# Causal masks written into PSUM ahead of the scores, 256 or 512 columns at a time, in the opening of an attention and SwiGLU kernel

## Chip, cores, metric

One core of one Trainium2 chip. The metric is the device time of one execution in microseconds. The kernel before takes 338.25 us (median of three runs, 337.61 to 338.68). All runs used below are marked fast, with a mean granted TensorE clock of 0.993 to 1.000 in the records.

## The reference, cut to what matters

```python
B, H, S, D = 8, 8, 576, 64
scores = (1 / sqrt(D)) * q @ k.T          # per batch and head
rel = pos[:, None] - pos[None, :]
scores = where((rel >= 0) & (rel < 64), scores, -1e9)
attn = softmax(scores) @ v
x = attn as (B*S, H*D) = (4608, 512)
out = (silu(x @ w_gate) * (x @ w_val)) @ w_out      # 512 -> 1536 -> 512
```

A query sees itself and the 63 keys before it. The kernel works in 36 groups of 128 tokens. For each half of a group (64 queries) it multiplies against 128 keys, and a mask removes the keys outside the window.

## The kernel before: the parts that matter

The scores of a group lie in two PSUM banks, one for the even and one for the odd heads (`a`); the two use the upper and the lower 64 rows of the TensorE array. In seven groups of the opening (0, 2, 3, 5, 4, 7, 6, in this order) the mask is added by TensorE (`masked=True`): a matmul of a 64x128 table of 0 and -1e30 against an identity. In the other 29 groups VectorE multiplies the exponentials by 0 and 1 instead.

```python
def scores(g, masked=False):
    ps = [ps_a.tile([P, 4, 2, 64], FP32, name="s_ps", tag="a") for _ in range(2)]
    for b in range(2):
        o = P * (g % 2) + 64 * b
        for p in range(4):
            for a in range(2):
                ...                                     # keys, rows y of half a
                nc.tensor.matmul(
                    ps[a][:, p, b], keys, qT[g // 2 % QR][y, p, o:o + 64],
                    tile_position=(64 * a, 0), start=True, stop=not masked)
            if masked:
                for a in range(2):
                    y = slice(64 * a, 64 * a + 64)
                    m = minus[1 if ORDER[g][1] == 0 and b == 0 else 0]
                    nc.tensor.matmul(
                        ps[a][:, p, b], m[y], identb[y, y],
                        tile_position=(64 * a, 0), start=False, stop=True)
...
def keys_last(n):                # VectorE; waits for the transposed keys (a DMA)
    b, i = ORDER[2 * n]
    if i is None:
        dve.tensor_copy(kL[:, :, b:b + 4, 64:P], kT[n % KR]...)
...
scores(0, True); scores(1); load_vg(1); ...; load_vg(2); load_vg(3)
... warm(7) ...                  # filler matmuls
# main loop, second half of an iteration
turn1(n + 4, "k_f"); keys_before(n + 4); keys_last(n + 4)
project(t - 1, s) ... step(t, 3 * s + 2)
```

The softmax here doesn't subtract the row's maximum and nothing guards it: scores larger than these inputs give would overflow.

## Time and profile before

| | before |
|---|---|
| median of three runs | 338.25 us |
| span of the profiled run | 336.9 us |
| TensorE matmuls, weight loads | 2825, 2825 |
| mask matmuls of 64 columns | 112 |

### The profile page before, as it was taken

The page shows a single profiled execution, that of the slowest core. Times are in us where ns is not written, and L with a number is a line of the kernel's source. Part 1 is how long each engine was busy: PE and PEld are TensorE (multiplying, and loading weights), DVE is VectorE, ACT ScalarE, POOL GpSimd, SP SyncE. Part 2 cuts the span into 40 slices and gives each one's busy share as a digit, 9 for nine tenths or more (in the row PEclk, how much of TensorE's full clock was granted, in tenths as well). Part 3 has the DMA queues.
Part 4 walks back from the last instruction along what each step waited for, and adds up shares of the span by engine and source line. Part 5 has one row for each costly group of instructions (what it writes and reads, how often), then busy time and mean ns, then how long its engine had stood idle before and what let it go on. Part 6 is the DMA issues. An engine that isn't in the chain of part 4 may idle for free.

```text
span 336.9 us, 7388 instructions
## 1 busy us (share of the span) xinstructions
PE 327.6 (97%) x2825; PEld 164.1 (49%) x2825; DVE 226.3 (67%) x491; ACT 151.9 (45%) x268; POOL 100.5 (30%) x148
## 2 busy tenths in 40 slices
PE   7898999999999999999999999999999999999996
PEld 3555665555544444444444444444444444444444
DVE  4657889895676666666676767766667766655520
ACT  3766876664634343434343443434343434233222
POOL 4444356660053333333333333223333200000000
DMA  8999999998978999798879798999787720211013
GB/s 209 247 312 264 280 301 326 322 185 194 228 137 149 192 151 190 151 193 162 181 151 194 137 195 174 158 179 181 158 180 157 104 62 34 65 31 31 33 47 109
DMA packets 150612, 56.85 MB, mean 169 GB/s; under 512 B 124721, under 2 KB 144561, under 8 KB 150577
## 3 DMA queue, kind: packets, MB, share of 16 engines
q1 hardware_dynamic: 150576, 56.38, 77.5%
q8 instruction: 22, 0.36, 0.5%
q14 instruction: 14, 0.11, 0.2%
HBM read 37.75 MB, written 9.44 MB: 140 GB/s over the span
## 4 chain that ended last, share of the span: by engine, by line
PE 87%; DMA 8%; SPq 3%; ACT 1%; POOL 0%; issue 0%; ACTq 0%; POOLq 0%
PE g_ps L309 27%; PE o_ps L327 27%; PE v_ps L309 26%; DMA q_f<-in_q_dram 6%; PE ao_ps L245 3%; PE s_ps L207 3%; DMA v_f<-in_v_dram 2%; SPq L110 1%; SPq L89 1%; PE tp L170 1%; DMA out_dram<-os__4994 1%; PE xtp L269 0%; POOL q_fb L120 0%; ACT q_fb L118 0%; ACT os__4994 L332 0%
## 5 line engine op out<-in xcount | busy, mean ns | idle before, releaser
L309 PE MATMUL g_ps<-xT,wg 128*128 128x512 bf16 (+1 forms) x460 | 112.4, 367 | 0.2
L309 PE MATMUL v_ps<-xT,wv 128*128 128x512 bf16 (+1 forms) x460 | 112.1, 366 | 0.5 <-ACT wv L118 0.5
L320 DVE SCALAR_TENSOR_TENSOR sg<-th,g_ps 128x512 f32<-128x512 f32 (+1 forms) x115 | 75.0, 652 | 53.8 <-ACT th L314 53.5
L314 ACT ACTIVATE th<-g_ps 128x512 f32<-128x512 f32 (+1 forms) x115 | 65.9, 573 | 76.4 <-PE g_ps L309 73.6
L327 PE MATMUL o_ps<-wo,hT 128*128 128x512 bf16 (+2 forms) x456 | 98.5, 368 | 0.0
L321 DVE TENSOR_TENSOR hT<-sg,v_ps 128x512 bf16<-128x512 f32 (+1 forms) x115 | 75.4, 656 | 11.9 <-PE xtp L269 0.5
L309 PEld LDWEIGHTS <-wv 128*128 128x128 bf16 x460 | 44.7, 98 | 49.4 <-ACT wv L118 1.0
L327 PEld LDWEIGHTS <-hT 128*128 128x128 bf16 x456 | 43.6, 98 | 49.5
L309 PEld LDWEIGHTS <-wg 128*128 128x128 bf16 x460 | 41.8, 98 | 42.3 <-issue 0.6
L227 ACT ACTIVATE E<-s_ps 128x512 bf16<-128x512 f32 x72 | 38.5, 596 | 8.0 <-PE s_ps L207 8.0
L120 POOL CAST q_fb<-q_f 128x1024 bf16<-128x1024 f32 x13 | 13.6, 1044 | 64.9 <-DMA q_f<-in_q_dram 41.2
L120 POOL CAST k_fb<-k_f 128x1024 bf16<-128x1024 f32 (+1 forms) x16 | 16.0, 1003 | 56.1 <-DMA k_f<-in_k_dram 46.1
L256 DVE TENSOR_TENSOR x_b<-ao_ps,r 128x256 bf16<-128x256 f32 x72 | 30.6, 425 | 2.5
L120 POOL CAST ve<-v_f 64x512 bf16<-64x512 f32 x47 | 28.9, 615 | 2.9
L229 DVE TENSOR_TENSOR E<-E,mask 128x512 bf16<-128x512 bf16 x58 | 23.3, 427 | 9.1 <-ACT E L227 8.3
L120 POOL CAST vo<-v_f 128x512 bf16<-128x512 f32 x30 | 18.9, 630 | 30.3 <-DMA v_f<-in_v_dram 30.1
L255 DVE RECIPROCAL r<-ao_ps 128x4 f32<-128x4 f32 x72 | 12.6, 174 | 5.4 <-PE ao_ps L245 5.3
L245 PEld LDWEIGHTS <-E 128*64 128x64 bf16 x576 | 11.0, 110 | 7.8 <-issue 5.7
L207 PEld LDWEIGHTS <-kT 64*128 64x128 bf16 x512 | 10.1, 95 | 6.6 <-issue 4.0
L120 POOL CAST vL<-v_f 64x512 bf16<-64x512 f32 x15 | 9.6, 638 | 10.2 <-DMA v_f<-in_v_dram 9.5
L207 PE MATMUL s_ps<-qT,kT 64*128 64x64 bf16 x512 | 12.2, 191 | 0.4 <-DVE x_b L256 0.3
L245 PE MATMUL ao_ps<-ve,E 128*64 128x65 bf16 x256 | 11.9, 196 | 0.1
(100 smaller groups left out, 150.1 us busy)
## 6 DMA issues: line engine op xcount, KB each, us to landing
v_f<-in_v_dram SPq DMA_DIRECT2D x32, 256.0 KB, 4.6
k_f<-in_k_dram SPq DMA_DIRECT2D x20, 256.0 KB, 4.1
q_f<-in_q_dram SPq DMA_DIRECT2D x18, 256.0 KB, 4.7
q_f<-in_q_dram SPq DMA_DIRECT2D x7, 512.0 KB, 7.0
k_f<-in_k_dram SPq DMA_DIRECT2D x6, 512.0 KB, 7.6
w_f<-in_moe_w_gate_dram SPq DMA_DIRECT2D x6, 512.0 KB, 6.2
w_f<-in_moe_w_val_dram SPq DMA_DIRECT2D x6, 512.0 KB, 6.5
wo_f<-in_moe_w_out_dram SPq DMA_DIRECT2D x6, 512.0 KB, 7.3
```

The costliest lines, as they stand in the source:

```text
L120: eng.tensor_copy(y, x)
L207: nc.tensor.matmul(ps[a][:, p, b], keys, qT[g // 2 % QR][y, p, o:o + 64], tile_position=(64 * a, 0), start=True, stop=not masked,)
L227: act.activation(e, x[:], AF.Exp, scale=0.125)
L229: dve.tensor_mul(e, e, mk[:].unsqueeze(1).to_broadcast([P, 4, 2, 64]))
L245: nc.tensor.matmul(o_ps[64 * b:64 * b + 64, i, :], Es[g % ER][:, y, b], z[:, y, :], tile_position=(0, 64 * b),)
L255: dve.reciprocal(r[:], o_ps[:, :, D])
L256: dve.tensor_mul(xb[g][:, 256 * h:256 * h + 256].rearrange("r (y d) -> r y d", y=4), o_ps[:, :, 0:D], r[:].unsqueeze(2).to_broadcast([P, 4 ...
L309: nc.tensor.matmul(ps[:, 0:n], w[:, c, P * m:P * m + P], xT[t][:, c, c0:c0 + n], start=(c == 0), stop=(c == 3),)
L314: act.activation(th[:, 0:n], g_ps[:, 0:n], AF.Tanh, scale=0.5)
L320: dve.scalar_tensor_tensor(sg[:, 0:n], th[:, 0:n], 1.0, g_ps[:, 0:n], ALU.add, ALU.mult)
L321: dve.tensor_mul(hT[t][:, m, c0:c0 + n], sg[:, 0:n], v_ps[:, 0:n])
L327: nc.tensor.matmul(o_ps[:, a:b], hT[t][:, c, P * s:P * s + P], wo[:, c, a:b], start=(c == 0), stop=(c == 11),)
```

## The change

Intent: fewer and wider mask matmuls. The mask goes into a whole bank first, for four heads at once, by repeating the identity block; the scores are added on top. It is one pair of 512 columns a group, or two pairs of 256 where the two halves have different masks (groups 0 and 4).

```diff
@@ scores(g, masked)
+        if masked:
+            first = ORDER[g][1] == 0
+            for b in range(2 if first else 1):
+                for a in range(2):
+                    y = slice(64 * a, 64 * a + 64)
+                    z, n = ps[a][:].rearrange("r p b x -> r (p b) x"), 8
+                    if first:
+                        z, n = ps[a][:, :, b], 4
+                    nc.tensor.matmul(
+                        z, minus[1 if first and b == 0 else 0][y],
+                        identb[y, y].unsqueeze(1).to_broadcast([64, n, 64]),
+                        tile_position=(64 * a, 0), start=(b == 0), stop=False,
+                    )
@@ the score matmul
-                        tile_position=(64 * a, 0), start=True, stop=not masked,
+                        tile_position=(64 * a, 0), start=not masked,
+                        stop=not masked or (b == 1 and p == 3),
@@
-                if masked:
-                    for a in range(2):
-                        ... (the 64-column mask matmul of before)
```

More of the change, by code (lines that the diff above doesn't have):

```diff
@@ L208, in scores @@
                         ps[a][:, p, b], keys, qT[g // 2 % QR][y, p, o:o + 64],
-                        tile_position=(64 * a, 0), start=True, stop=not masked,
-                    )
-                if masked:
-                    for a in range(2):
-                        y = slice(64 * a, 64 * a + 64)
-                        m = minus[1 if ORDER[g][1] == 0 and b == 0 else 0]
-                        nc.tensor.matmul(
-                            ps[a][:, p, b], m[y], identb[y, y], tile_position=(64 * a, 0),
-                            start=False, stop=True,
-                        )
+                        tile_position=(64 * a, 0), start=not masked,
+                        stop=not masked or (b == 1 and p == 3),
+                    )
         sps[g] = ps, masked
```

## The prediction

> **What bounds the kernel now.** I read the page first (busy shares and the row of slices), to see which engine sets the pace where.
>
> ```profile
> PE 327.6 (97%) x2825; PEld 164.1 (49%) x2825; DVE 226.3 (67%) x491; ACT 151.9 (45%) x268; POOL 100.5 (30%) x148
> PE   7898999999999999999999999999999999999996
> DMA  8999999998978999798879798999787720211013
> PE 87%; DMA 8%; SPq 3%; ACT 1%; POOL 0%; issue 0%; ACTq 0%; POOLq 0%
> ```
>
> TensorE is busy 97% of the span and the chain that ended last lies on it for 87%. The rest of the chain is nearly all DMA (8% and 3% for the issuing queue). Only the first four slices (8.4 us each, so up to about 34 us) have gaps on PE. "Opening" in the change is exactly this stretch, so next I cut the span at PE's last wait, which the timeline puts at 34.55 us. The columns are the stretch, its length, then the busy time of PE, PEld, DVE, ACT and POOL.
>
> ```profile
> 0.00:34.55 34.55, 28.35 (x421) 16.61 (x421) 21.20 (x69) 21.58 (x39) 15.67 (x32) 1.00 1.01 258
> 34.55:40.90 6.35, 6.26 (x110) 4.25 (x111) 5.40 (x10) 5.50 (x10) 2.89 (x4) 1.00 1.02 271
> 40.90:60.00 19.10, 19.10 (x183) 11.07 (x182) 17.12 (x37) 13.71 (x26) 9.92 (x12) 1.00 1.13 313
> ```
>
> Before 34.55 us PE has 6.2 us of holes, afterwards practically none. DMA is at its full share throughout the opening. The waits of PE (total, times, longest), taken over the first 45 us, say what the holes are:
>
> ```profile
> PE w_ps L340 <- DVE wz L344: 1.3, 1, 1.3
> PE tp L170 <- DVE q_fb L120: 1.0, 1, 1.0
> PE tp L170 <- POOL k_fb L120: 0.9, 2, 0.7
> PE tp L170 <- ACT q_fb L118: 0.9, 1, 0.9
> PE xtp L269 <- ACT E L227: 0.6, 1, 0.6
> PE v_ps L309 <- ACT wv L118: 0.5, 1, 0.5
> PE s_ps L207 <- DVE x_b L256: 0.3, 1, 0.3
> ```
>
> They are waits for casts of freshly loaded data. None is a wait for a mask. So what PE saves before such a hole makes the hole longer and does not move the end; what it saves after 34.55 us, where PE runs dense to the end of the kernel, comes off one for one. That is the sorting rule for everything below.
>
> Then the instructions that the change touches, listed by their tile. First the two kinds (lines 207 and 215), then a piece of the timeline of the last masked pair of groups (start us, length us):
>
> ```profile
> L207 PE MATMUL s_ps<-qT,kT x512: 187/190/200, 8.6 to 260.5; 64*128 64x64 bf16 x171
> L215 PE MATMUL s_ps<-identb,minus x112: 188/190/200, 8.6 to 40.6; 64*128 64x64 bf16 x112
> ```
>
> ```profile
> 40.23 0.19 PE L215 MATMUL s_ps<-identb,minus 64*128 64x64 bf16 x2
> 40.26 0.19 PE L207 MATMUL s_ps<-qT,kT 64*128 64x64 bf16 x2
> ...
> 40.60 0.19 PE L207 MATMUL s_ps<-qT,kT 64*128 64x64 bf16 x2
> 40.63 0.19 PE L215 MATMUL s_ps<-identb,minus 64*128 64x64 bf16 x2
> 40.76 0.61 PE L309 MATMUL g_ps<-xT,wg 128*128 128x256 bf16 x4
> ```
>
> The reader must not take the 190 ns for the cost. It is a latency; the cost is the distance of starts. From 40.23 to 40.63 there are 14 steps of one pair (two matmuls on the two row halves of the array, "x2"): 0.40/14 = 29 ns a pair. Two matmuls of 64 columns thus pass in 29 ns: the two row halves run at the same time, and the pairs follow with no hole, weight loads included. For 512 columns on the whole array the distance is read in the same timeline: four matmuls of the gate start at 41.64 and the next four at 42.51, 0.87/4 = 217 ns each; 256 columns: 41.21 to 41.64, 0.43/4 = 108 ns each.
>
> **What the Trainium skill says.** "TensorE: Matmul & The Clock Gate", section "Back-to-back issue gap", gives N/2.4 + 2.5 ns for a warm stream: 29.2 ns for 64 columns, 109 for 256, 216 for 512. The trace agrees at all three (29, 108, 217). That section's table also lists about 60 cycles for anything of 1 to 64 columns, with an issue floor of about 25 ns; 29 ns a pair is above that floor, so 64 columns is not a size where the floor is what is paid. Same page, section "Packing small matmuls — row/col tiling": matmuls on different row groups overlap, their starts some 4 ns apart. The 29 ns pair agrees. "PSUM — Partial Sum Buffer", section "The four PSUM rules": the first matmul of a group clears the accumulate bits of the whole bank, and a later one without that flag overwrites where the bit is clear and adds where it is set. That is what makes one flag for a bank's four heads correct in the new order; it promises no speed, and no run here shows it yet.
>
> **The change part by part.** Seven groups are masked this way: 0, 2, 3, 5, 4, 7, 6 (7 groups x 16 = the 112 of the row).
> - Removed: 112 mask matmuls of 64 columns with 112 weight loads, that is 56 pairs, 56 x 29 = 1.62 us of PE flow.
> - Added: for groups 2, 3, 5, 7, 6 one pair of 512 columns each, 5 x 217 = 1.08 us if the halves overlap; for groups 0 and 4 (first of a sequence, two different masks) two pairs of 256 each, 4 x 108 = 0.43 us. 18 matmuls and 18 loads, 1.51 us in sum.
> - The columns streamed are the same: 112 x 64 = 7168 = 10 x 512 + 8 x 256. Only the fixed part of about 2.5 ns a pair goes: 56 pairs become 9. So the gain is about 1.62 - 1.51 = 0.11 us, 16 ns a group. The weight loads lay beside the streaming already (29 ns a pair with a 95 ns load), so 94 fewer are worth nothing by themselves.
> - Moved: the masks now come before the scores, so they need only the two constants and a free PSUM bank. POOL finishes the last constant that they need at 3.76 us (timeline), the first mask runs at 8.6. Group 0: between its second and third score pair I see starts at 8.62 and 8.75 with a mask pair at 8.65, so one hole of about 0.07 us while the second half of the query copy ends on DVE (8.70). Masks in front fill it: 0.07 us more. Group 3: its first score starts at 15.61 and the second at 16.16, held by the normalising multiply that frees the second bank. Afterwards the first bank's 512-column mask runs inside that wait, but the second bank's runs alone after it: 217 + 8 x 29 = 0.45 us from the release, against 16 x 29 = 0.46 before. No change.
> - Unchanged: every score matmul, the exponentials, the PSUM banks taken and their order, the DVE and ACT work, all transfers.
>
> What lies on the path: groups 0, 2, 3 (8.6 to 16.6 us) are followed by holes at 12.65, 17.35 (0.6 us, for an exponential that ACT begins after a cast of late data), 26.0 and 27.9; their 0.07 + 3 x 0.016 = 0.12 us is lost there. Groups 5 and 4 (29.3 to 30.2) are followed by the 0.5 us hole at 34.55, for a weight cast that starts on ACT when its DMA lands; 0.03 us is lost there. Only groups 7 and 6 (39.7 to 40.7) come after the last hole: 2 x 16 = 0.03 us at the end. The sum is -0.03 us on the path, at most -0.2 us if nothing were absorbed. Against 338.25 that is 0.01 to 0.06%, below the 1.07 us spread of the three runs before.
>
> **The rivals.**
> 1. "94 matmuls fewer at 190 ns." The table of groups by form gives the mask matmuls 4.1 us of busy time, and 94 of the 112 go: 94/112 x 4.1 = 3.4 us. If that came off the end, 334.8 us, still only 1.0%. Against it: the busy time is made of latencies, the flow is 29 ns a pair, and five of the seven groups lie ahead of holes.
> 2. The long row-tiled pair doesn't overlap (the second half waits for the first to finish, because the moving operand is a repeated 64-column block, or the long stream hogs the port). Then each group's masks cost twice: +1.51 us of PE work, 7 x 0.216. By the same rule groups 7 and 6 put 0.43 us on the path and the holes swallow most of the rest: 338.6, at worst 339.7 us. For it: no long row-tiled pair exists in this trace. Against it: short ones overlap fully, and the operands are of the same kind.
> 3. A new wait: the first score of a group after a long mask into the same bank must wait until that has drained (about 0.17 us, from 0.379 us latency less 0.217 of flow). 7 x 0.17 = 1.2 us, 0.34 on the path: 338.6. Against it: today a mask lands on columns 29 ns after the score that wrote them, without a hole.
> 4. The slightly shifted opening reorders buffer releases and so transfers. DMA is at full share there, and the chain of the first 38 us is DMA of q and v and the queue that issues it. The opening's end could move by some tenths either way: +-0.5 us. Against: PE frees no staging buffer by these instructions; ACT, DVE and POOL do.
>
> **Range and chances.** Centre: 338.25 - 0.03 = 338.2 us. The spread of the three runs (-0.64, +0.43) and rivals 2 to 4 (up to +0.4 likely, +1.5 worst) give 337.3 to 339.2 as eight in ten. 2% is 6.8 us: all the masked groups' mask flow is 1.6 us, so neither side is reachable by any of these sums. Faster 1%, within 98%, slower 1%.
>
> **What would show each step.** In the profile after, PE and PEld have 2731 instructions instead of 2825. The mask line has 18 matmuls, 8 of 256 and 10 of 512 columns. In groups 7 and 6 the second matmul of a mask pair starts within some ns of the first and the first score some 0.22 us after it, so a group takes about 0.45 instead of 0.47 us; if starts are 0.22 us apart, rival 2 holds; if the first score starts 0.35 us or more after the mask, rival 3. The holes before the transposes and at 34.55 us stay, each longer by at most 0.1 us. The dense flow after 40.9 us starts some hundredths earlier. PE busy falls by less than 0.3 us although 94 instructions go. The prediction is wrong if the time leaves 337.3 to 339.2 in fast runs, or if the holes ahead of 34.55 us change by more than the saved tenth, which would mean that the opening hangs on these matmuls after all.

## More of the kernel before

The lines on which the argument rests are quoted in the prediction. Two views that it did not use turned out to matter. The first is the DMA queue table of the page. I read the queue named "instruction" as the one that brings TensorE's own instructions:

```profile
q8 instruction: 22, 0.36, 0.5%
```

In the trace each of these 22 packets has 16,384 bytes. TensorE has 5650 matmuls and weight loads, some 257 for each packet. The second view is the list of ScalarE's waits from 12 to 17 us (line, what it waited for, total, times, longest):

```profile
ACT ve L118 <- DMA v_f<-in_v_dram: 0.9, 1, 0.9
ACT vL L118 <- DMA v_f<-in_v_dram: 0.4, 1, 0.4
```

ScalarE casts loaded blocks of v here, and the exponentials of groups 2 and 3 stand behind these casts.

## The result, and the profile after

The changed kernel takes 338.03 us (median of 6 runs, 337.58 to 338.25); the kernel before, in the same rounds and those earlier, 337.95 us. The ratio of fast runs is 0.9999 with a 95% interval of 0.9986 to 1.0012: the same. (Ratios are the mean time of one kernel's fast runs over that of the other's fast runs of the same rounds, so not quite the ratio of the medians quoted.)

The busy row of the page after, its instruction queue, and the mask line of the list by tile (duration in ns: least, median, most; then first and last start in us):

```profile
PE 326.8 (97%) x2731; PEld 163.3 (49%) x2731; DVE 227.5 (68%) x491; ACT 152.0 (45%) x268; POOL 100.8 (30%) x148
q8 instruction: 21, 0.34, 0.5%
L208 PE MATMUL s_ps<-identb,minus x18: 269/377/387, 8.6 to 38.8; 64*128 64x512 bf16 x10, 64*128 64x256 bf16 x8
```

94 matmuls and 94 weight loads are gone, as predicted. TensorE's busy time falls by 0.8 us; less than 0.3 was predicted. (Busy time differs by 0.5 us between `before` and `order_kl`, which have the same number of matmuls, so this says little.) The timeline of groups 7 and 6 after (start us, length us):

```profile
38.35 0.39 PE L208 MATMUL s_ps<-identb,minus 64*128 64x512 bf16 x2
38.57 0.40 PE L221 MATMUL s_ps<-qT,kT 64*128 64x64 bf16 x16
38.80 0.38 PE L208 MATMUL s_ps<-identb,minus 64*128 64x512 bf16 x2
39.02 0.40 PE L221 MATMUL s_ps<-qT,kT 64*128 64x64 bf16 x16
39.35 0.61 PE L316 MATMUL g_ps<-xT,wg 128*128 128x256 bf16 x4
```

The two long matmuls pass in 0.22 us together (38.35 to 38.57), so the halves overlap, and the scores follow at once. The two groups take 1.00 us to the next gate matmul (38.35 to 39.35). Before it was 1.04 us (39.72 to 40.76). That is the predicted 0.02 us a group.

But the prediction said that they would start some hundredths earlier, and they start 1.37 us earlier. To see where this comes from and where it goes I lined up the 115 tanh activations of all traces by their order; each follows a group of gate matmuls, so it shows TensorE's progress. Given is the lead against the first trace of before (negative is earlier):

| trace | tanh 1 (21.2 us) | tanh 9 (39.4) | tanh 13 (45.6) | tanh 91 (257.6) | tanh 96 (270.3) |
|---|---|---|---|---|---|
| before, again | +0.05 | -0.24 | -0.23 | -0.23 | -0.23 |
| after | -0.72 | -1.37 | -1.41 | -1.41 | -0.60 |
| after, again | -0.82 | -1.33 | -1.36 | -1.36 | -0.85 |

From 46 to 257 us the lead is constant to 0.01 us: dense TensorE work. Near 260 us the changed kernel loses 0.5 to 0.8 us at a single place. The lead does not grow steadily before that: 0.7 to 0.8 us are there at 21 us, but at tanh 4 (24.7 us) both traces of the changed kernel are 0.14 and 0.26 us *behind*, and at tanh 5 (29.0 us) 0.67 and 0.62 us ahead. And the first trace of before comes from an execution of 338.57 us, 0.6 us above the median, so a lead against it overstates a typical gain by about that. Still, there were two effects that my prediction didn't have.

**Where the lead begins.** ScalarE's waits after, same stretch of 12 to 17 us:

```profile
ACT vL L118 <- DMA v_f<-in_v_dram: 0.2, 1, 0.2
```

The wait of 0.9 us is gone: the third load of v lands at 14.14 us instead of 15.19. The packets on the instruction queue (read from the trace one by one) say why. Before, a fetch of 16,384 bytes ran at 12.0 us, for 1.3 us, while that load was in flight; after, with 24 TensorE instructions fewer in group 0, the fetch comes at 15.9 us.

This alone can hardly be the gain, since against the first trace the lead is gone at 24.7 us. What lasts longer is what happens to the loads behind. SyncE issues them one after the other (start us, length us), before and then after:

```profile
11.37 2.34 SPq L284 DMA_DIRECT2D w_f<-in_moe_w_gate_dram  x1
13.75 0.84 SPq L284 DMA_DIRECT2D w_f<-in_moe_w_val_dram  x1
15.80 0.61 SPq L89 DMA_DIRECT2D k_f<-in_k_dram  x1
```

```profile
11.37 1.01 SPq L291 DMA_DIRECT2D w_f<-in_moe_w_gate_dram  x1
12.42 0.74 SPq L291 DMA_DIRECT2D w_f<-in_moe_w_val_dram  x1
14.47 0.91 SPq L89 DMA_DIRECT2D k_f<-in_k_dram  x1
```

The issue that was under way during the fetch took 1.3 us longer, and the four loads behind it were issued 1.3 to 1.4 us later. The DMA engines then had less to do. What they moved from 14 to 20 us, before and then after:

```profile
DMA packets 1919, 1.74 MB, mean 291 GB/s; under 512 B 269, under 2 KB 1919, under 8 KB 1919
DMA packets 2167, 2.01 MB, mean 335 GB/s; under 512 B 274, under 2 KB 2166, under 8 KB 2166
```

The missing 0.27 MB takes 0.8 us at 335 GB/s (an estimate from these two lines).

**Where it is lost.** VectorE's timeline near 259 us, before and then after, with TensorE's wait after:

```profile
256.07 0.86 DVE L138 COPY kL<-kT 128x256 bf16<-128x256 bf16 x1
259.07 0.43 DVE L145 COPY kL<-kT 128x1024 bf16<-128x1024 bf16 x1 [2.14 <-DMA kT<-k_fb]
```

```profile
254.66 0.88 DVE L138 COPY kL<-kT 128x256 bf16<-128x256 bf16 x1
258.98 0.43 DVE L145 COPY kL<-kT 128x1024 bf16<-128x1024 bf16 x1 [3.44 <-DMA kT<-k_fb]
259.33 0.68 DVE L327 SCALAR_TENSOR_TENSOR sg<-th,g_ps 128x512 f32<-128x512 f32 x1
```

```profile
260.06 1.02 PE L316 MATMUL g_ps<-xT,wg 128*128 128x512 bf16 x4 [0.76 <-DVE sg L327]
```

The copy of the last keys waits for two DMA transposes. The gate product `sg` stands behind it on VectorE and starts only about when the copy ends (259.33 us), though its tanh was done at 256.8 us; with `sg` waits the PSUM buffer that TensorE's next gate needs. Everything before that copy is 1.4 us earlier after than before; the copy itself is not. The DMA view from 256.0 to 257.6 us, first before, then after (issues: how many, us to landing):

```profile
kT<-k_fb SPq DMA_TRANSPOSE x2, 2.5
```

```profile
q8 instruction: 1, 0.02, 5.3%
...
out_dram<-os__4134 SPq DMA_DIRECT2D x1, 256.0 KB, 3.2
kT<-k_fb SPq DMA_TRANSPOSE x1, 3.8
```

After, an instruction fetch falls on the second transpose, which takes 3.8 us instead of 2.5. Before, the neighbouring fetches were at 244.5 and 261.9 us. A store of results (`out_dram`) is issued in this window too, 1.36 us after the second transpose; before, the corresponding store follows at 1.35 us, so it is not what differs.

### The profile page after: what moved, and what is told of

It is laid out like the page before. It is cut to its first block, busy times and chain, and to the rows that moved or that the text cites. A ratio compares the mean times of both kernels' runs of the same rounds, so it can differ in the third digit from the quotient of the medians.

```text
span 336.3 us, 7201 instructions
## 1 busy us (share of the span) xinstructions
PE 326.8 (97%) x2731; PEld 163.3 (49%) x2731; DVE 227.5 (68%) x491; ACT 152.0 (45%) x268; POOL 100.8 (30%) x148
## 4 chain that ended last, share of the span: by engine, by line
PE 85%; DMA 7%; ACT 2%; DVE 2%; SPq 1%; issue 1%; DVEq 0%; ACTq 0%
PE g_ps L316 26%; PE o_ps L334 26%; PE v_ps L316 25%; DMA q_f<-in_q_dram 3%; PE ao_ps L252 3%; PE s_ps L221 2%; DMA v_f<-in_v_dram 2%; PE tp L170 1%; DMA kT<-k_fb 1%; ACT E L234 1%; SPq L89 1%; DMA out_dram<-os__4900 1%; DVE sg L327 1%; PE xtp L276 1%; ACT ve L118 0%
## 5 line engine op out<-in xcount | busy, mean ns | idle before, releaser
L328 DVE TENSOR_TENSOR hT<-sg,v_ps 128x512 bf16<-128x512 f32 (+1 forms) x115 | 75.4, 655 | 11.9 <-PE xtp L276 0.5
L236 DVE TENSOR_TENSOR E<-E,mask 128x512 bf16<-128x512 bf16 x58 | 25.8, 472 | 9.0 <-ACT E L234 8.3
L221 PEld LDWEIGHTS <-kT 64*128 64x128 bf16 x512 | 9.1, 95 | 5.7 <-issue 3.0
L252 PE MATMUL ao_ps<-vo,E 128*64 128x65 bf16 x256 | 11.9, 196 | 0.0
L252 PE MATMUL ao_ps<-ve,E 128*64 128x65 bf16 x256 | 11.9, 196 | 0.0
## 6 DMA issues: line engine op xcount, KB each, us to landing
v_f<-in_v_dram SPq DMA_DIRECT2D x32, 256.0 KB, 4.5
k_f<-in_k_dram SPq DMA_DIRECT2D x20, 256.0 KB, 4.1
q_f<-in_q_dram SPq DMA_DIRECT2D x18, 256.0 KB, 5.1
```

The source lines that it names most:

```text
L221: nc.tensor.matmul(ps[a][:, p, b], keys, qT[g // 2 % QR][y, p, o:o + 64], tile_position=(64 * a, 0), start=not masked, stop=not masked or ...
L236: dve.tensor_mul(e, e, mk[:].unsqueeze(1).to_broadcast([P, 4, 2, 64]))
L252: nc.tensor.matmul(o_ps[64 * b:64 * b + 64, i, :], Es[g % ER][:, y, b], z[:, y, :], tile_position=(0, 64 * b),)
L328: dve.tensor_mul(hT[t][:, m, c0:c0 + n], sg[:, 0:n], v_ps[:, 0:n])
```

## The experiments

My theory after the result: the masks themselves are worth what I predicted (some hundredths); the two larger effects come from the *number* of TensorE instructions, which moves every later instruction fetch, and a fetch holds up a transfer in flight. The rivals: the order of masks and scores matters; or the whole lead is run-to-run scatter; or the loss near 260 us is not the fetch, but simply what happens to any kernel that arrives early.

### The two kernels again

> A control: the kernel before, unchanged, against itself. My theory (the masks' flow shrinks by 16 ns a group and only two groups lie behind the last hole) says that the 1.4 us by which the changed kernel's trace leads at the score groups 7 and 6 is the opening's run-to-run scatter of landings, so this second trace of before should start groups 7 and 6 anywhere between 38 and 40.5 us, not again at 39.7. The rival (the masks ahead really do shorten the opening by 1.4 us and something gives it back) says 39.7 us within 0.2. Ratio 1.000 within 0.0015 in any case.

Measured: 338.16 us, ratio 0.9999 (0.9972 to 1.0026). Groups 7 and 6 start at 39.49 us, 0.23 from the first trace. My expectation of scatter up to 38 us was not met.

> The changed kernel once more. Ratio 0.9999 within 0.0015. My theory: groups 7 and 6 start anywhere between 38 and 40.5 us; a group of 16 scores and one long mask pair takes 0.45 us. The rival of a real lead: 38.35 us within 0.2 again, and again a wait of the gate for DVE later.

Measured: 338.10 us, ratio 0.9992 (0.9968 to 1.0015). They start at 38.40 us (38.35 in the first trace of after), and the wait for VectorE near 260 us is there again, 0.5 us. So the rival of a real lead was right: it is not only scatter.

### Order alone, width alone

`order_only`: masks ahead of the scores, but of 64 columns each (112 matmuls).

```diff
-            for b in range(2 if first else 1):      # one long pair, or two
+            for b in range(2):
+                for p in range(4):                  # 8 pairs of 64 columns
+                    ... matmul(ps[a][:, p, b], m[y], identb[y, y],
+                               start=(b == 0 and p == 0), stop=False)
```

> Masks ahead of the scores, but as 56 pairs of 64 columns (half of the change: the order). My theory: groups 7 and 6 take 16 x 29 = 0.46 to 0.47 us each, as before; group 0 loses its 0.07 us hole; time 338.0, ratio 1.000 within 0.0015. The rival that the old interleaving cost something (a mask onto columns just written) says 0.45 or less per group with 64 columns too.

Measured: 338.17 us, ratio 0.9995 (0.9969 to 1.0020). Groups 7 and 6 take 1.04 us (40.07 to 41.11), as before. The fetch is at 12.3 us, the third v lands at 15.34. There is no lead (+0.34 at tanh 9) and no loss near 260 us.

`width_only`: scores first, then the long masks on top (one clearing flag at a bank's first score).

```diff
-    masks (long), then scores
+    scores with start=(b == 0 and p == 0), then masks (long) with start=False
```

> The long masks behind the scores (the other half: the width; one accumulate flag at the first score of a bank, results correct). My theory: groups 7 and 6 take 8 x 29 + 217 = 0.45 us each, 0.02 less than before; group 0 keeps its small hole for the query copy; time 338.0, ratio 1.000 within 0.0015. If the changed kernel's order matters, this one is slower than it by some tenths.

Measured: 338.08 us, ratio 0.9995 (0.9972 to 1.0019). Groups 7 and 6 take 1.01 us (38.98 to 39.99). The fetch is at 16.1 us, the third v lands at 14.02, the lead at tanh 1 is 0.78 us, and 0.83 us are lost near 260 us (-0.77 to +0.06). The times can't tell the four kernels apart. The traces can: the landing of the third v and the loss near 260 us go with the width, that is with the count of instructions, and neither with the order. (At tanh 5 the `order_only` trace leads by 0.92 us; it has lost that by tanh 8. The opening scatters that much.)

### Moving the fetch

`after_warm13`: one filler matmul of 512 columns behind group 0 cut into 13 of 39 columns, which puts back the 24 instructions that group 0 lost.

```diff
-    warm(7)
+    warm(6)
+    for i in range(13):
+        nc.tensor.matmul(w_ps[:, 39 * i:39 * i + 39], wz[:, 0:P], wz[:, 0:39])
```

> The changed kernel with one warming matmul of 512 columns behind group 0 cut into 13 of 39 columns: 12 matmuls and 12 weight loads more ahead of 11 us, exactly what the change took out of group 0 (16 mask matmuls became 4), for some 0.1 us of filler. Theory (fetch): the opening's lead comes from a 16,384-byte instruction fetch that ran at 12.0 us in the kernel before and delayed the third load of v (landed 15.1 to 15.3), and that runs at 15.9 us in the changed one (landed 14.0 to 14.1). With the 24 instructions back: a fetch at 12 us, the third v lands at 15.0 to 15.4, the first tanh at 21.0 to 21.5 instead of 20.4. Rival (the masks themselves): fetch or not, v lands at 14.1 and the first tanh stays at 20.4. Time ratio within 0.002 of 1 either way.

Measured: 338.32 us, ratio 0.9999 (0.9960 to 1.0037). The fetch came at 13.1 us, not at 12.0, because the added instructions stand later than the masks did. It missed the third v (14.00) and hit the fourth, which landed at 16.46 instead of 15.2. ScalarE's waits from 12 to 17 us in that kernel:

```profile
ACT vL L118 <- DMA v_f<-in_v_dram: 1.5, 1, 1.5
```

TensorE then waits for ScalarE's exponential at 17 us again, as before:

```profile
17.65 0.38 PE L276 MATMUL xtp<-identb,x_b 128*128 128x128 bf16 x4 [0.90 <-ACT E L234]
```

Nothing about the masks differs from the changed kernel, so the fetch moves the landing of v and this wait. The first tanh, at 22.78 us, is later still, and that is not the fetch alone: TensorE's granted clock was halved from 18.7 to 22.1 us in this trace (in the row, behind the five engines: clock, DMA share, GB/s), and no other of the fourteen traces shows this in its opening.

```profile
18.70:22.10 3.40, 3.40 (x36) 1.95 (x36) 2.08 (x8) 1.77 (x4) 2.46 (x3) 0.50 1.13 323
```

Nor does the delay last: the lead is -0.55 us at tanh 9. The fetch hit a later issue here (1.85 us instead of 0.54), and the DMA engines moved 335 GB/s from 14 to 20 us, as in the changed kernel. The times do not settle it either: three of the six executions show a mean clock of 0.993 to 0.995 and take 338.40 to 339.73 us, the three with full clock 337.20 to 338.24. So this run shows what the fetch does to landings, not that it brings the old time back.

`after_halves`: 96 gate and value matmuls of 512 columns, between 80 and 105 us, cut in two of 256.

```diff
-    matmul(ps[:, 0:n], w[...], xT[t][:, c, c0:c0 + n], start=(c == 0), ...)
+    for h in range(2):                                # first 12 steps of the loop
+        matmul(ps[:, k * h:k * h + k], w[...], xT[t][:, c, c0 + k * h:...],
+               start=(c == 0 and h == 0), ...)
```

> The changed kernel with 96 gate and value matmuls of 512 columns (the first 12 whole steps of the loop, about 80 to 105 us) cut into two of 256: 192 instructions more, against the 188 that the change removed; cost 96 x 2.5 = 0.24 us of PE flow. Theory (fetch): instruction fetches after that run where they ran in the kernel before (near 243 and 260 us instead of 239 and 256), the two key transposes at 254 to 257 us land 2.4 us after their issue (3.8 in the changed kernel's second), and the gate's wait of 0.5 to 0.8 us for DVE near 262 us is gone, so that the lead at the end is 1.1 us or so instead of 0.6 to 0.85; time 337.6 to 337.9. Rival (the wait comes from the lead itself, the transposes' data being late): the slow landing and the wait stay, time 338.3.

Measured: 337.45 us, ratio 0.9973 (0.9939 to 1.0006); before in these rounds 337.99 us. The fetches are at 244.5 and 261.3 us, as in the kernel before. The transposes near 255 us take 2.4 to 2.5 us, and the wait for VectorE is gone. The added matmuls cost 0.24 us (lead -0.88 at 60 us, -0.64 at 130 us), and 0.64 us of lead remain to the end; I had expected 1.1. Another 0.7 us were lost between tanh 9 and 13 (39 to 46 us), ahead of the cut matmuls, which I have not traced. A kernel with *more* TensorE work is thus by median some 0.6 us faster than the changed one, each against before of its own rounds (-0.54 against +0.08 us; its interval just includes 1).

### Taking the key copy out of the way

`kl_after` and `kl_before`: the copy of the last keys called half an iteration later, in the changed kernel and in the one before.

```diff
     keys_before(n + 4)
-    keys_last(n + 4)
 ...                                   # next iteration, first half
     step(t, 3 * s + 2)
+    keys_last(n + 3)
```

> The changed kernel with the DVE copy of the last keys (which waits for the transposes) called half an iteration later, where nothing behind it is urgent. Theory: the slow transpose near 255 us is still slow (it is the fetch's doing), but DVE no longer stands before it with the gate's product behind, so PE's wait for DVE near 262 us is gone and the opening's lead of 1.36 to 1.41 us at the score groups 7 and 6 reaches the end: profiled span about 335.3, time 337.2 to 337.6, ratio 0.998. Rival (something else in that place bounds): the wait turns up under another name and time stays 338.0.

Measured: 337.19 us, ratio 0.9960 (0.9924 to 0.9997); before 337.99 us by median. The slow transpose is still there (issued at 255.42, landed at 259.38, a fetch at 256.4), but the copy finds its data ready, TensorE has no wait there, and the lead of 1.07 us (1.36 to 1.41 expected) is the same at tanh 13 and at tanh 96.

> The kernel before with the same later copy. Theory: it had no wait of PE there, so nothing is gained: ratio 1.000 within 0.0015. If this one gains as much as the changed kernel does with it, the gain has nothing to do with the fetch.

Measured: 338.04 us, ratio 1.0004 (0.9963 to 1.0046): nothing gained, as expected. (Its one trace leads by 0.63 us from the opening; a single trace is that uncertain.) So on the same chip, with the place near 260 us defused in both, the changed kernel is 0.85 us faster by median (337.19 against 338.04), and all six of its executions (336.65 to 337.51) lie below all six of the other (from 337.93). That is what it gains in the opening. Without the later copy it gives about the same back (+0.08 and +0.06 us against before in its own two sets of rounds).

### How few instructions it takes

`order_kl` is `order_only` with the later key copy; `g0_kl` is that with the long masks in group 0 alone.

```diff
+            if g == 0:  masks long (4 matmuls of 256 columns)
+            else:       masks of 64 columns (16 matmuls)
```

> The later key copy, masks ahead of the scores, but all of 64 columns: all that the fastest version so far (kl_after, 337.19 us) has, with the 188 PE instructions back. PE flow is only 0.1 us more. Theory (fetch: the count of instructions does it): a fetch near 12 us, the third v lands at 15.1 to 15.4, time 337.8 to 338.2. Rival (the order of masks and scores does it): 337.2 as kl_after.

Measured: 338.04 us, ratio 0.9996 (0.9976 to 1.0015), fetch at 11.9 us, third v at 15.22.

> As order_kl, but group 0's masks alone are long: 24 instructions fewer ahead of the first fetch, worth about 0.02 us of PE flow. Theory (fetch): the first fetch moves from 12 to 15 us or later, the third v lands at 14.0 to 14.2 and the fourth at 15.1 to 15.4, the first tanh at 20.3 to 20.6, and most of the gain is there: 337.1 to 337.6. Rival (long masks in all groups are needed): 338.0.

Measured: 337.06 us, ratio 0.9968 (0.9951 to 0.9985), fetch at 15.6 us, third v at 14.06, fourth at 15.16, first tanh at 20.41 us. ScalarE's waits from 12 to 17 us, first in `order_kl`, then in `g0_kl`:

```profile
ACT ve L118 <- DMA v_f<-in_v_dram: 0.9, 1, 0.9
ACT vL L118 <- DMA v_f<-in_v_dram: 0.3, 1, 0.3
```

```profile
ACT vL L118 <- DMA v_f<-in_v_dram: 0.2, 1, 0.2
```

24 instructions in one group bring 1.0 us by median (338.04 to 337.06, same chip, same rounds; one of the six executions of `order_kl`, 337.02, is as fast as those of `g0_kl`, so single executions overlap). The long masks of the other six groups add nothing that these runs can show. `g0_kl` and `kl_after` are the two fastest versions; they ran on different chips, so which is faster is open. (The profiled run of `g0_kl`, 338.05 us, is the slowest of its six, so its trace is not typical in the later opening: it leads by 0.53 us at tanh 13.)

### What masks cost, enlarged

Both start from `kl_after` and put the long masks of some groups five times, which changes no result.

```diff
-            for b in range(2 if first else 1):
+            for b, r in [(b, r) for b in ... for r in range(5 if g in GROUPS else 1)]:
```

> kl_after with the long masks of groups 7 and 6 put five times each (results unchanged in effect): 8 more pairs of 512 columns behind the last hole. By the prediction's sorting rule all of it reaches the end: 8 x 0.217 = 1.74 us, so 337.2 + 1.7 = 338.9 (338.5 to 339.4 with other fetch times). The trace: 4 x 0.217 = 0.87 us more between the first mask of a group and its first score, if the halves overlap; 1.74 us a group and 340.7 in all, if they don't.

Measured: 339.43 us, ratio 1.0038 (1.0018 to 1.0057). Groups 7 and 6 in that timeline:

```profile
38.28 1.25 PE L208 MATMUL s_ps<-identb,minus 64*128 64x512 bf16 x10
39.37 0.40 PE L221 MATMUL s_ps<-qT,kT 64*128 64x64 bf16 x16
39.60 1.24 PE L208 MATMUL s_ps<-identb,minus 64*128 64x512 bf16 x10
40.68 0.40 PE L221 MATMUL s_ps<-qT,kT 64*128 64x64 bf16 x16
```

Five pairs take 1.09 us (38.28 to 39.37), 0.218 us a pair: the halves overlap. The two groups take 2.73 us to the next gate instead of 1.01 in `kl_after`, 1.72 us more, and the lead falls by about as much (from -1.44 at tanh 9 to +0.25 at tanh 13): what is added behind the last hole reaches the end. The time is 0.03 us above my bracket, and 2.2 us above `kl_after` (another chip), 2.4 above `g0_kl` of the same rounds: 0.37 us more are lost between 46 and 88 us, and I have not traced those.

> kl_after with the masks of groups 0, 2, 3, 5 and 4 put five times each: 5 x 4 x 0.217 = 4.3 us more PE flow ahead of the last holes. By the sorting rule the holes (0.95 us at 12.7, 1.1 at 27, 0.2 to 0.5 twice near 33) swallow most: 0.9 + 1.1 + 0.7 = 2.7 us swallowed, some 1.6 us left: 338.8 (337.8 to 339.6). Rival (nothing is swallowed, the opening hangs on PE): 341.5.

Measured: 338.62 us, ratio 1.0020 (0.9999 to 1.0040). Twenty pairs' worth of masks, 4.3 us of TensorE flow, cost 1.4 us against `kl_after` (another chip) or 1.6 against `g0_kl` of the same rounds. TensorE's waits over the first 45 us, beside the first one for the zeroed filler:

```profile
PE tp L170 <- POOL k_fb L120: 0.5, 1, 0.5
PE tp L170 <- ACT q_fb L118: 0.5, 1, 0.5
PE tp L170 <- DVE q_fb L120: 0.3, 1, 0.3
```

They add up to 1.3 us; in `kl_after` the same list has 3.8 us. The holes swallow more than half, although this kernel's fetch also hit the fourth v (13.2 us; landed 16.63).

### All traces together

| traces | first TensorE fetch, us | third v lands | fourth v lands | first tanh |
|---|---|---|---|---|
| before, before_again, order_only, order_kl, kl_before | 11.9 to 12.3 | 15.14 to 15.34 | 16.17 to 16.48 | 21.18 to 21.50 |
| after, after_again, width_only, after_halves, kl_after, g0_kl, late_x5 | 15.6 to 16.1 | 14.02 to 14.21 | 15.15 to 15.36 | 20.36 to 20.54 |
| after_warm13, early_x5 | 13.1, 13.2 | 14.00, 14.03 | 16.46, 16.63 | 22.78 (half clock), 21.64 |

In the seven traces whose first fetch comes before 14 us, the load that SyncE was issuing while it ran took 1.2 to 1.4 us longer to issue than the same load in the other seven. From 14 to 20 us the DMA engines moved 262 to 319 GB/s in the five traces of the first row and 332 to 335 in the nine others. Shortly before tanh 5 TensorE transposes the third load of q; that lands at 26.3 to 26.6 us in the nine and at 26.3 to 27.7 in the five.

And for the key transposes after 90 us, in all fourteen traces: of 235 with no fetch in flight between 0.8 us after issue and landing, the median landed 2.43 us after issue and the slowest 2.62. Of 35 with one of TensorE's fetches in flight the median is 3.32 us, the slowest 4.32, and 23 lie above 2.6; the 12 others met the fetch only in their last 0.3 us. Of 9 with one of the shorter fetches (8,192 bytes) of the other instruction queue, 2 lie above 2.6. (The 0.8 us is my choice.) A store of results in flight is not a rival cause: 107 of the 235 had one, with a median of 2.42 us.

## Why the prediction was right, point by point

- **The time and the class: right.** 338.2 was predicted, 338.03 measured, ratio 0.9999.
- **The flow of the masks: right.** 0.02 us a group (1.04 to 1.00 us for two). Rival 1, busy time for cost, fell. Rival 2, no overlap, fell: 0.22 us a long pair, 0.218 in the enlarged form. Rival 3, a drain before the first score, fell: the score starts 0.22 us after the mask.
- **The sorting rule: right in the main.** Behind the last hole 1.72 us more on TensorE came through in full, with 0.5 to 0.7 us on top that are not explained; ahead of the holes 4.3 us became some 1.5.
- **Group 3: right.** Its second bank still waits for VectorE, 0.2 us, and the first bank's mask runs inside that wait.
- **"Unchanged: ... all transfers", and that 94 fewer weight loads are worth nothing by themselves: wrong.** This is the step that failed. The count of instructions moves the fetches, and these move transfers: in the opening the third v lands 1.05 us earlier and four loads are issued 1.3 to 1.4 us earlier, near 256 us the second key transpose takes 1.3 us longer. The opening brings 0.85 us (`kl_after` against `kl_before`), the second takes about as much back. The predicted time was met because these two cancel, not because nothing happened: that was luck.
- **"Each hole longer by at most 0.1 us" and "some hundredths earlier": wrong.** The wait for ScalarE's exponential at 17 us (0.6 us) vanished, the hole at 34.55 us (0.49 us) shrank to 0.17, and groups 7 and 6 started 1.37 us earlier (1.1 against the second trace of before). By the prediction's own test the opening does react, though to a fetch and not to TensorE's work.
- **Rival 4 came nearest.** It allowed the opening to move by some tenths through transfers, but looked for the cause in the release of buffers.
- **Three readings were loose.** "DMA is at its full share throughout the opening": from 14 to 16 us its share was 0.83 before and 1.17 after (219 and 308 GB/s), the stretch to which the gain is put down above. The list of waits lacks one row (0.4 us for a cast of k on VectorE), and of its seven rows four are casts of loaded data; the others are the zeroed filler, an exponential and the normalised x. And the skill's section gives the formula that the sum uses for an isolated matmul, not for a sustained stream; the traces bear out its sizes all the same (last section).

What stays open: the exact path from the late issues at 12 to 16 us to the lead at 40 us. That the smaller amount moved by 20 us is the gain is argued from its size (0.8 us) and from the grouping of the traces, and no run puts the fetch back at 12 us in the changed kernel. Other fetches moved too (from 33.2 to 34.6 us, from 41.6 to 45.5), and traces with the old instruction count differ among themselves by 1.2 us at tanh 13 (-0.63 to +0.56); I did not separate these. That the changed kernel's loss near 260 us happens in its unprofiled executions as well is argued from the medians, not seen.

## What to carry to other kernels

When a change removes instructions and hardly any work, look at where the instruction fetches fall, before and after: in this opening, which waits for landings, 24 instructions fewer moved one fetch by 4 us and brought some 50 times the work that they save (1.0 us against an estimated 0.02). Look also at what stands behind a wait for a DMA on the same engine: moving one copy by half an iteration made this kernel indifferent to a transfer that lands 1.5 us late. And an unchanged time is not an unchanged kernel: line up the same events of several traces before saying that nothing happened.

## What the Trainium skill lacked or had wrong

- "Runtime: NRT & Kernel Launch", section "Instruction fetch mechanics", gives the blocks of 16 KiB, 256 instructions, and calls the cost of crossing into the next one mostly hidden. The block size agrees (packets of 16,384 bytes, 22 for TensorE's 5650 matmuls and weight loads, 21 for 5462). What it lacks is what the fetch does to others: it takes 0.9 to 1.9 us as one packet, data transfers in flight land up to 1.9 us late (key transposes 2.43 us without, up to 4.32 us with one), and SyncE's issue of a load under way takes 1.2 to 1.4 us longer (2.34 us instead of 1.01). Through that it cost 0.5 to 0.8 us of TensorE time at one place, while no wait of TensorE was put down to the fetch itself.
- "TensorE: Matmul & The Clock Gate", section "Back-to-back issue gap", gives about 131 ns a matmul of 512 columns as a sustained figure beside the 216 ns of its formula. Here only the formula holds: four of them take 0.87 us, 217 ns each, in the densest stretches.
- The same section's table has about 60 cycles for anything of 1 to 64 columns. A pair of 64-column matmuls on two row halves passes every 29 ns here, 4 above the table's floor, and the cost is nearly in proportion to the length (29 ns for 64 columns, 217 for 512, a factor of 7.5 for 8). Making the masks wider saved 0.02 us a group. No run has single matmuls of 64 columns on the whole array, so the table's row itself was not tested.
